# Keys and queries of a head group through one transposing transfer per token tile, and re-ordered first batches with causal masks added by TensorE

## The chip, the cores and the metric

The kernel runs on one core of a Trainium2 chip. The metric is the device time of one execution in microseconds; lower is better. In the profile PE is TensorE (PEld its weight loads), DVE VectorE, ACT ScalarE, POOL GpSimd, and SP the engine that issues most of the transfers. SPq and ACTq are the transfers issued by SP's and by ScalarE's queue. Each engine runs its instructions in program order.

## What is computed

Inputs: q, k, v of shape (8, 8, 576, 64): batches, heads, tokens, head width; s of shape (8, 8, 576); weights of 512 x 2048 and 2048 x 512.

```python
scores = scale * np.matmul(q, k.transpose(0, 1, 3, 2))
causal = np.triu(np.ones((S, S), dtype=bool), k=1)
cum = np.cumsum(np.maximum(s, 0.0), axis=-1)
bias = -(cum[:, :, :, None] - cum[:, :, None, :])
scores = np.where(causal, -1000000000.0, scores + np.minimum(bias, 0.0))
attn = softmax(scores)
x = matmul(attn, v)                  # heads side by side: (8, 576, 512)
xn = (x - mean) / sqrt(var + 1e-6) * g_ln
out = x + relu(xn @ w_ch1) @ w_ch2
```

## The kernel before

**Work.** There are 64 heads, n = 0 to 63 (n = 8 b + h). A head's scores are made transposed, keys on partitions, in three banks of 512 columns that hold only the blocks on and under the causal diagonal (`scores`, L300 to L336: tiles sa, sb, sc); the last block of 64 tokens is made for two heads at once (`scores_d`, tile sd). ScalarE takes Exp of each bank into the tile er (L314, L349). GpSimd then zeroes the upper half of each of the four diagonal blocks with an affine select (L328), and of the last block (L352). `pv` multiplies er with v and a column of ones (tile pot), and VectorE divides by the sum (L387 to L396). Layer norm (`ln_stats`, `ln_aggr`, `ln_xn`, `ln_tr`) and the two layers of the MLP (`mlp1`, tile ph, L467; `mlp2`, tile py, L485) of one batch run as 32 units between the heads of the next. The last 64 tokens of each batch are collected two batches to a tile (xm) for a last, mixed chunk.

**The bias by four more rows.** The contraction has 68 rows instead of 64: the cumulative sum, split into three bf16 parts c_hi, c_mid, c_lo, stands beside the keys, with ones beside them in the queries, and -c_hi beside the queries with ones in the keys.

**Keys and queries, two ways.** A group gam is 4 heads, half a batch; kT and qT have two buffers, used by groups in turn.
- Batches 0 and 1 (`NPE = 2`, groups 0 to 3): `load_qk` loads a pair of heads, `cast` makes bf16, `qk_pair` transposes on TensorE into PSUM (L261), and four copies take it to kT and qT (L113, VectorE). `aug` writes the bias rows with four small transfers.
- Batches 2 to 7 (groups 4 to 15): `ld_rows` loads token rows of a group (L213), `cast_rows` makes bf16 rows of 68 columns and 60 zeros on GpSimd (L230, L231), and `tr_rows` (L243) sends each tile of 128 or 64 tokens through a transposing transfer: one for K and one for Q for each of five token tiles, 512 columns each. The four parts of a group (K tiles 0 to 2, Q tiles 0 to 2, K tiles 3 and 4, Q tiles 3 and 4) are sent in the four heads before the group's first.

**Order.** Everything is written out by hand. In each head n: `pre(n)` (loads, casts and transposes due in this head), `qk_pair` where due, `scores(n)`, one MLP unit, `scores_d` on even heads, another unit, `pv(n-1)`, layer norm pieces, the rest of the units. Before the first head stands a setup: loads, fills, the cumulative sum, the first pair. The MLP starts with head 10, after the casts of its weights (`cast_w1` on VectorE, L160; `cast_w2` on GpSimd). SP issues loads, transposes and the output's stores in one queue, in program order; a transpose waits for its rows' cast, a store for its sum yo (L494), a load for a free buffer of its pool (2 each for K and Q, 3 for v).

Of the kernel before, what the change touches and what calls it, by code (L numbers as in the profile page):

```python
# [15 lines left out]
P = 128  # L16
# [3 lines left out]
def kernel(  # L20
# [26 lines left out]
    G = 4  # L47
    NPE = 2
    PARTS = ((0, 1, 2), (3, 4))
# [4 lines left out]
    stage = ctx.enter_context(tc.tile_pool(name="stage", bufs=2))  # L54
    pairs = ctx.enter_context(tc.tile_pool(name="pairs", bufs=3))
# [14 lines left out]
    ident = const.tile([P, P], BF16, name="ident")  # L70
    w1_bf = const.tile([P, KD, Dh], BF16, name="w1_bf")
# [5 lines left out]
    qT = [const.tile([P, G, SP], BF16, name=f"qT{i}") for i in range(2)]  # L77
    kT = [const.tile([P, G, SP], BF16, name=f"kT{i}") for i in range(2)]
    er = const.tile([P, 4, EW], BF16, name="er")
    rows = [const.tile([P, G, P], BF16, name=f"rows{i}") for i in range(6)]  # L80
    cTk = const.tile([P, NT, BH, 4], BF16, name="cTk")
    cTq = const.tile([P, NT, BH, 4], BF16, name="cTq")
    xm = [const.tile([P, Dm], F32, name=f"xm{i}") for i in range(4)]
    xTm = const.tile([P, KD, 512], BF16, name="xTm")
    ones4 = const.tile([G, S], BF16, name="ones4")
# [3 lines left out]
    c_neg = const.tile([BH, S], BF16, name="c_neg")  # L89

    def load_qk(src, b, j, name):
        tmp = stage.tile([P, 2, QT * D], F32, name=name, tag=name)
        nc.sync.dma_start(
            out=tmp[0:QP],
            in_=src[b, 2 * j : 2 * j + 2].rearrange("h (p t) d -> p h (t d)", t=QT),
        )
        return tmp

    def load_v(b, t):
        pn = P if t < NF else TL
        tmp = stage.tile([P, H, D], F32, name="vtmp", tag="vtmp", bufs=3)
        nc.sync.dma_start(
            out=tmp[:pn], in_=v[b, :, t * P : t * P + pn, :].rearrange("h s d -> s h d")
        )
        return tmp
# [8 lines left out]

    loaded = {}
    ready = {}

    def ld(kind, b, i):  # L120
        if b >= B:
            return
        if kind == "v":
            loaded["v", b, i] = load_v(b, i)
        else:
            loaded[kind, b, i] = load_qk(k if kind == "k" else q, b, i, kind + "tmp")

    def cast(kind, b, i, eng):
        if b >= B:
            return  # L130
        tmp = loaded.pop((kind, b, i))
        if kind == "v":
            pn = P if i < NF else TL
            copy_on(eng, v_bf[b % 2][:pn, i, :, 0:D], tmp[:pn])
        else:
            t = pairs.tile([P, QT, 2, D], BF16, name=kind + "p", tag=kind + "p")
            copy_on(
                eng,
                t[0:QP].rearrange("p t h d -> p h t d"),
                tmp[0:QP].rearrange("p h (t d) -> p h t d", d=D),  # L140
            )
            ready[kind, b, i] = t
# [32 lines left out]
    def cum_tile(name):  # L175
        return yop.tile([P, S], F32, name=name, tag="yo")

    def aug(b, g, eng):
        r0 = b * H + g * G
        i = (b * 2 + g) % 2  # L180
        for j, src in enumerate((c_hi, c_mid, c_lo)):
            eng.dma_start(out=kT[i][D + j : D + j + 1, :, 0:S], in_=src[r0 : r0 + G, :])
        eng.dma_start(out=qT[i][D + 3 : D + 4, :, 0:S], in_=c_neg[r0 : r0 + G, :])

    def bias_rows():
# [7 lines left out]
        for t0, t1, pn in ((0, NF, P), (NF, NT, TL)):  # L196
            nc.vector.tensor_copy(
                out=cTk[0:pn, t0:t1, :, 0:3],
                in_=tr[0:pn, :, t0:t1, :].rearrange("p j t x -> p t x j"),
            )  # L200
            nc.vector.tensor_scalar_mul(
                out=cTq[0:pn, t0:t1, :, 3], in0=tr[0:pn, 0, t0:t1, :], scalar1=-1.0
            )

    def ld_rows(kind, gam, part):
        if gam >= 2 * B:
            return
        src = k if kind == "k" else q
        b, h0 = gam // 2, (gam % 2) * G
        tmp = stage.tile([P, 3, G, D], F32, name=kind + "tmp", tag=kind + "tmp")  # L210
        for u, t in enumerate(PARTS[part]):
            pn = P if t < NF else TL
            nc.sync.dma_start(  # L213
                out=tmp[0:pn, u],
                in_=src[b, h0 : h0 + G, t * P : t * P + pn, :].rearrange("h s d -> s h d"),
            )
        loaded[kind, gam, part, "rows"] = tmp

    turn = [0]

    def cast_rows(kind, gam, part):
        if gam >= 2 * B:
            return
        tmp = loaded.pop((kind, gam, part, "rows"))
        got = []
        for u, t in enumerate(PARTS[part]):
            pn = P if t < NF else TL
            r = rows[turn[0] % 6]
            turn[0] += 1
            nc.gpsimd.tensor_copy(out=r[0:pn, :, 0:D], in_=tmp[0:pn, u])  # L230
            nc.gpsimd.tensor_copy(  # L231
                out=r[0:pn, :, D:KA],
                in_=(cTk if kind == "k" else cTq)[0:pn, t, gam * G : (gam + 1) * G, :],
            )
            got.append((t, pn, r))
        ready[kind, gam, part, "rows"] = got

    def tr_rows(kind, gam, part):
        if gam >= 2 * B:
            return  # L240
        dst = (kT if kind == "k" else qT)[gam % 2].rearrange("p h s -> p (h s)")
        for t, pn, r in ready.pop((kind, gam, part, "rows")):
            nc.sync.dma_start_transpose(  # L243
                out=dst[:, t * G * P : t * G * P + G * pn].rearrange(
                    "p (h s) -> p h s", h=G
                ),
                in_=r[0:pn].rearrange("p h c -> p (h c)"),
            )


    def qk_pair(b, j, engs=("dve", "dve", "dve", "dve")):
        if b >= B:
            return
# [3 lines left out]
        for kind, dst in (("k", kT), ("q", qT)):  # L257
            src = ready.pop((kind, b, j))
            tr = ps_t.tile([P, S], BF16, name="trqk", tag="tr")
            for t in range(QT):  # L260
                nc.tensor.transpose(  # L261
                    tr[:, t * QP : (t + 1) * QP],
                    src[0:QP, t, :, :],
                    ident[0:QP, 0:QP],
                )
            for u in range(2):
                copy_on(
                    engs[n],
                    dst[i][0:D, hh + u, 0:S].rearrange("d (p t) -> d p t", t=QT),
# [3 lines left out]

    def e_of(b, h):
        return er, h % 4


    def k_cols(b, h, kb):
        i, hh = (b * 2 + h // G) % 2, h % G
        if b < NPE:  # L280
            return kT[i][0:KA, hh, kb * P : (kb + 1) * P]
        n = P if kb < NF else TL
        o = kb * G * P + hh * n
        return kT[i].rearrange("p h s -> p (h s)")[0:KA, o : o + P]

    def q_cols(b, h, q0, q1):
        i, hh = (b * 2 + h // G) % 2, h % G
        if b < NPE:
            return [(q0, q1, qT[i][0:KA, hh, q0:q1])]
        flat = qT[i].rearrange("p h s -> p (h s)")  # L290
        got = []
        if q0 < NF * P:
            full = flat[0:KA, 0 : NF * G * P].rearrange("p (t h s) -> p t h s", t=NF, h=G)
# [242 lines left out]
    for t in range(3):  # L536
        ld("v", 0, t)
# [252 lines left out]
```

## Time and profile before

| | |
|---|---|
| median of three runs | 471.72 us (471.6 to 472.0) |
| profiled execution | 468.62 us |
| its span, first to last instruction | 466.9 us |
| mean granted TensorE clock | 0.893 |
| TensorE busy | 371.4 us (80%) |
| VectorE, ScalarE, GpSimd busy | 213.3, 175.4, 193.2 us |
| read from memory, written | 36.85 MB, 9.44 MB |

A row of a group reads: line, engine, operation, output and input tiles, shapes, count | busy time in us, mean ns of one | idle time of the engine before it, and what ended it. A row in order of time reads: start in us, duration, engine, line, operation, tiles, count [idle before, what ended it]. In the row of a transposing transfer grouped by line stand minimum, median and maximum in ns. A window's row reads: stretch, length, busy time (instructions) of PE, PEld, DVE, ACT and POOL, granted clock, share of the 16 transfer engines, GB/s. In the slices each digit is a tenth of busy time in a fortieth of the span; PEclk is the granted clock in tenths.

### The profile page before, as it was taken

What the parts mean: (1) busy time and instruction counts of PE and PEld (TensorE: products, weight loads), DVE (VectorE), ACT (ScalarE), POOL (GpSimd) and SP (SyncE); (2) the same over time, 40 slices, a digit from 0 to 9 for tenths busy, and PEclk for the clock granted to TensorE, in tenths of its full rate; (3) what the DMA queues carried; (4) which work ended last, traced back from release to release, by engine and by line L of the source; (5) the groups of instructions that cost most, each with busy time, mean ns of one, the idle gap of its engine ahead of it and who ended that gap; (6) DMA issues with size and microseconds to landing.
All of it is one profiled execution on the core that took longest, in us unless ns stands there. A gap on an engine that the chain in (4) does not pass through costs nothing. (4 is left out here: it accounts for less than half of the span.)

```text
span 466.9 us, 8307 instructions
## 1 busy us (share of the span) xinstructions
PE 371.4 (80%) x2848; PEld 200.3 (43%) x2895; DVE 213.3 (46%) x525; ACT 175.4 (38%) x339; POOL 193.2 (41%) x609
## 2 busy tenths in 40 slices
PE   1486469917979984999299939896699899999995
PEld 0264335504535542555155515453355455444442
DVE  7579777523714640447024712473145526511211
ACT  4252225603337242643255325532272463050320
POOL 3274516835646625554446545543466222000000
PEclk9975559987979995999789977999599999999999
DMA  7885078985877487665866586549765600101102
GB/s 201 216 249 138 13 251 241 217 181 137 191 146 139 97 176 169 115 129 119 189 135 132 117 196 131 117 103 174 162 133 107 137 2 22 69 0 46 46 23 68
DMA packets 167578, 61.09 MB, mean 131 GB/s; under 512 B 155624, under 2 KB 158768, under 8 KB 167536
## 3 DMA queue, kind: packets, MB, share of 16 engines
q1 hardware_dynamic: 167456, 60.51, 57.1%
q8 instruction: 23, 0.38, 0.4%
q14 instruction: 19, 0.16, 0.1%
q10 hardware_dynamic: 80, 0.05, 0.0%
HBM read 36.85 MB, written 9.44 MB: 99 GB/s over the span
## 5 line engine op out<-in xcount | busy, mean ns | idle before, releaser
L485 PE MATMUL py<-w_bf,hT 128*128 128x512 bf16 x554 | 135.6, 382 | 1.5 <-DVE yo L494 0.4
L467 PE MATMUL ph<-xT,w_bf 128*128 128x512 bf16 x488 | 130.3, 403 | 2.1 <-ACT hT L477 0.5
L328 POOL TENSOR_SCALAR_AFFINE_SELECT er<-er 128x128 bf16<-128x128 bf16 x256 | 73.4, 303 | 87.4 <-ACT er L314 86.9
L314 ACT ACTIVATE er<-sa 128x512 bf16<-128x512 f32 x64 | 38.1, 596 | 166.1 <-PE sa L305 107.3
L477 ACT ACTIVATE hT<-ph 128x512 bf16<-128x512 f32 x108 | 64.5, 597 | 91.9 <-PE ph L467 90.8
L467 PEld LDWEIGHTS <-w_bf 128*128 128x128 bf16 x576 | 53.9, 101 | 58.1 <-issue 11.3
L475 DVE TENSOR_SCALAR hT<-ph 128x512 bf16<-128x512 f32 x36 | 24.9, 692 | 113.7 <-PE ph L467 112.2
L305 PEld LDWEIGHTS <-kT 68*128 68x128 bf16 x464 | 35.8, 105 | 95.2 <-issue 38.2
L305 PE MATMUL sa<-qT,kT 68*128 68x512 bf16 x64 | 27.8, 434 | 60.2 <-DMA qT<-rows 47.3
L485 PEld LDWEIGHTS <-hT 128*128 128x128 bf16 x576 | 51.9, 98 | 50.2 <-issue 2.0
L379 PEld LDWEIGHTS <-er 128*128 128x128 bf16 x960 | 42.7, 105 | 17.9 <-issue 5.2
L379 PE MATMUL pot<-v_bf,er 128*128 128x65 bf16 x960 | 45.1, 203 | 3.2 <-POOL v_bf L115 2.5
L230 POOL CAST rows<-qtmp 128x256 bf16<-128x256 f32 (+1 forms) x60 | 24.1, 401 | 46.8 <-issue 25.1
L387 DVE RECIPROCAL rinv<-pot 128x5 f32<-128x5 f32 x64 | 12.4, 193 | 61.2 <-PE pot L379 61.0
L494 DVE TENSOR_TENSOR yo<-py,xb 128x512 f32<-128x512 f32 x32 | 22.0, 689 | 39.5 <-PE py L485 39.3
L314 ACT ACTIVATE er<-sc 128x512 bf16<-128x512 f32 x64 | 38.9, 608 | 0.0
L314 ACT ACTIVATE er<-sb 128x512 bf16<-128x512 f32 x64 | 38.2, 596 | 1.8 <-PE sb L305 0.7
L230 POOL CAST rows<-ktmp 128x256 bf16<-128x256 f32 (+1 forms) x60 | 23.9, 399 | 25.7 <-DMA kT<-rows 17.3
L305 PE MATMUL sb<-qT,kT 68*128 68x384 bf16 (+2 forms) x176 | 28.4, 269 | 2.5 <-DMA qT<-rows 2.3
L305 PE MATMUL sc<-qT,kT 68*128 68x256 bf16 (+1 forms) x224 | 28.5, 249 | 0.0
L389 DVE TENSOR_TENSOR xb<-pot,rinv 128x256 f32<-128x256 f32 x64 | 27.2, 424 | 2.2
L438 DVE TENSOR_SCALAR xn<-xb,mv,rs 128x512 bf16<-128x512 f32 x32 | 20.6, 704 | 9.7 <-POOL rs L425 9.7
(71 smaller groups left out, 289.8 us busy)
## 6 DMA issues: line engine op xcount, KB each, us to landing
vtmp<-in_v_dram SPq DMA_DIRECT2D x32, 256.0 KB
out_dram<-yo SPq DMA_DIRECT2D x32, 256.0 KB
ktmp<-in_k_dram SPq DMA_DIRECT2D x48, 128.0 KB
qtmp<-in_q_dram SPq DMA_DIRECT2D x48, 128.0 KB
w1tmp<-in_moe_w_ch_dram SPq DMA_DIRECT2D x8, 512.0 KB
w2tmp<-in_moe_w_ch_dram SPq DMA_DIRECT2D x8, 512.0 KB
ktmp<-in_k_dram SPq DMA_DIRECT2D x8, 288.0 KB
qtmp<-in_q_dram SPq DMA_DIRECT2D x8, 288.0 KB
```

Of the source, the lines that this page charges most:

```text
L230: nc.gpsimd.tensor_copy(out=r[0:pn, :, 0:D], in_=tmp[0:pn, u])
L305: nc.tensor.matmul(dst[:, a0 - q0 : a1 - q0], lhsT=k_cols(b, h, kb), rhs=cols, start=True, stop=True,)
L314: nc.scalar.activation(out=e[:, u, o : o + 512], in_=a, func=ACT.Exp, scale=scale)
L328: nc.gpsimd.affine_select(out=e[:, u, o : o + P], in_=e[:, u, o : o + P], compare_op=ALU.is_ge, fill=0.0, base=0, pattern=[[1, P]], channe ...
L379: nc.tensor.matmul(pot[:, t, :], lhsT=e[:, u, o : o + P], rhs=vv[:, kb, h, :], start=(kb == 0), stop=(kb == last),)
L389: nc.vector.tensor_tensor(out=xb[b][:, :, hs], in0=pot[:, 0:NF, 0:D], in1=rinv[:, 0:NF].unsqueeze(2).to_broadcast([P, NF, D]), op=ALU.mult,)
L438: nc.vector.tensor_scalar(out=xn, in0=x, scalar1=mv[:, t, 0:1], scalar2=rs[:, t : t + 1], op0=ALU.subtract, op1=ALU.mult,)
L467: nc.tensor.matmul(ph, lhsT=w1_bf[:, kd, fb * P : (fb + 1) * P], rhs=xT[:, kd, :], start=(kd == 0), stop=(kd == KD - 1),)
L475: nc.vector.tensor_scalar_max(out=hT[:, fb, :], in0=ph, scalar1=0.0)
L477: nc.scalar.activation(out=hT[:, fb, :], in_=ph, func=ACT.Relu)
L485: nc.tensor.matmul(py[0], lhsT=hT[:, fb, t * P : (t + 1) * P], rhs=w2_bf[:, fb, :], start=(fb == 0), stop=(fb == FB - 1),)
L494: nc.vector.tensor_add(out=yo, in0=py[0], in1=x)
```

## The change

1. kT and qT become one tile kq (K and Q side by side), and rows become tiles of K and Q side by side. One transfer per token tile transposes 1024 columns: five a group instead of ten. Row loads stay (one for K, one for Q per tile). GpSimd casts K and Q in one instruction, and copies the four bias columns of both in another. The transposes of a group are spread over the heads -4, -3 and -2 before its first (group 4: -3, -2, -1).
2. In the first ten heads (`NM = 10`) TensorE adds -1e30 above the diagonal by a product of the identity with a mask tile, four for each head, and the four affine selects of these heads go.
3. The first batches are re-ordered: one staging pool of six buffers for all loads; casts of pairs and of v almost all on GpSimd; one of the four pair copies on ScalarE; constant rows of ones and minus ones filled instead of transferred (c_hi is used for both operands, c_neg goes); the bias transfers of group 1 move from ScalarE's queue to SP's, that of g_ln from SP's to ScalarE's; an Exp of two numbers at the start.

```diff
+    NM = 10
+    NR = 4
-    stage = ctx.enter_context(tc.tile_pool(name="stage", bufs=2))
-    pairs = ctx.enter_context(tc.tile_pool(name="pairs", bufs=3))
+    stage = ctx.enter_context(tc.tile_pool(name="stage", bufs=6))
+    pairs = ctx.enter_context(tc.tile_pool(name="pairs", bufs=2))
...
+    kq = [const.tile([P, 2, G, SP], BF16, name=f"kq{i}") for i in range(2)]
-    rows = [const.tile([P, G, P], BF16, name=f"rows{i}") for i in range(6)]
+    rows = [const.tile([P, 2, G, P], BF16, name=f"rows{i}") for i in range(NR)]
...
+    def ld_rows(gam, t):
+        pn = P if t < NF else TL
+        b, h0 = gam // 2, (gam % 2) * G
+        tmp = stage.tile([P, 2, G, D], F32, name="rowtmp", tag="st")
+        for u, src in enumerate((k, q)):
+            nc.sync.dma_start(
+                out=tmp[0:pn, u],
+                in_=src[b, h0 : h0 + G, t * P : t * P + pn, :].rearrange("h s d -> s h d"),
+            )
+        loaded["rows", gam, t] = tmp
...
+    def cast_rows(gam, t):
...
+        nc.gpsimd.tensor_copy(out=r[0:pn, :, :, 0:D], in_=loaded.pop(("rows", gam, t))[0:pn])
+        nc.gpsimd.tensor_copy(
+            out=r[0:pn, :, :, D:KA], in_=cT[0:pn, t, :, gam * G : (gam + 1) * G, :]
+        )
...
+    def tr_rows(gam, t):
+        pn = P if t < NF else TL
+        r = ready.pop(("rows", gam, t))
+        o = t * 2 * G * P
+        nc.sync.dma_start_transpose(
+            out=kq[gam % 2]
+            .rearrange("p u h s -> p (u h s)")[:, o : o + 2 * G * pn]
+            .rearrange("p (h s) -> p h s", s=pn),
+            in_=r[0:pn].rearrange("p u h c -> p (u h c)"),
+        )
...
+    def aug(gam, eng):
+        r0 = gam * G
+        i = gam % 2
+        eng.dma_start(out=kq[i][D + 1 : D + 2, 0, :, 0:S], in_=c_hi[r0 : r0 + G, :])
+        eng.dma_start(out=kq[i][D : D + 1, 1, :, 0:S], in_=c_hi[r0 : r0 + G, :])
+        eng.dma_start(out=kq[i][D + 2 : D + 3, 0, :, 0:S], in_=c_mid[r0 : r0 + G, :])
+        eng.dma_start(out=kq[i][D + 3 : D + 4, 0, :, 0:S], in_=c_lo[r0 : r0 + G, :])
...
+        pe_mask = b * H + h < NM
+        def bank(name, blocks, o):
...
+                if pe_mask and diag:
+                    nc.tensor.matmul(
+                        a[:, c : c + P], lhsT=ident, rhs=maskT, start=False, stop=True
+                    )
+            nc.scalar.activation(out=e[:, o : o + 512], in_=a, func=ACT.Exp, scale=scale)
...
+        if pe_mask:
+            return
         for o in (0, OB + 64, OC, OC + 320):
             nc.gpsimd.affine_select(
...
+    nc.scalar.activation(out=warm[:, 1:2], in_=warm[:, 0:1], func=ACT.Exp)
+    nc.scalar.dma_start(out=gln, in_=moe_g_ln.rearrange("(kd p) -> p kd", p=P))
+    nc.gpsimd.memset(kq[0][D : D + 1, 0].bitcast(F32), NEG2)
+    nc.vector.memset(kq[0][D:KA, 1].bitcast(F32), ONE2)
...
+    cast_pair("k", 0, 0, "act")
+    cast_pair("q", 0, 0, "pool")
+    ld_v(0, 2)
+    ld_v(0, 3)
...
+    qk_pair(0, 0, ("act", "dve", "act", "dve"))
+    aug(0, nc.scalar)
+    cast_pair("k", 0, 1, "pool")
+    cast_pair("q", 0, 1, "pool")
+    ld_v(0, 4)
+    ld_pair("k", 0, 2)
+    ld_pair("q", 0, 2)
+    cast_v(0, 0, "act")
+    cast_v(0, 1, "pool")
+    ld_pair("k", 0, 3)
+    ld_pair("q", 0, 3)
     for i in range(2):
         nc.gpsimd.memset(v_bf[i][:, 0:NF, :, D : D + 1], 1.0)
...
+    cast_v(0, 2, "pool")
+    cast_v(0, 3, "pool")
+    cast_v(0, 4, "pool")
+    nc.gpsimd.memset(kq[1][D : D + 1, 0].bitcast(F32), NEG2)
+    nc.gpsimd.memset(kq[1][D:KA, 1].bitcast(F32), ONE2)
+    nc.gpsimd.memset(kq[1][0:KA, 0, :, S:SP], 0.0)
+    aug(1, nc.sync)
...
+        if n == 0:
+            cast_pair("k", 0, 2, "pool")
+            cast_pair("q", 0, 2, "pool")
+            ld_pair("k", 1, 0), ld_pair("q", 1, 0)
+            ld_v(1, 0), ld_v(1, 1)
...
+        lead = {2 * NPE: 1}
+        for gam in range(2 * NPE, NG):
+            m = n - 4 * gam - lead.get(gam, 0)
+            if m == -6:
+                ld_rows(gam, 0), ld_rows(gam, 1)
+            elif m == -5:
+                cast_rows(gam, 0), cast_rows(gam, 1)
+                ld_rows(gam, 2), ld_rows(gam, 3)
+            elif m == -4:
+                tr_rows(gam, 0), tr_rows(gam, 1)
+                cast_rows(gam, 2), cast_rows(gam, 3)
+                ld_rows(gam, 4)
+            elif m == -3:
+                tr_rows(gam, 2), tr_rows(gam, 3)
+                cast_rows(gam, 4)
+            elif m == -2:
+                tr_rows(gam, 4)
...
         if n >= 17:
+            if 1 <= h < 6:
+                ld_v(b + 1, h - 1)
+            if 2 <= h < 7:
+                cast_v(b + 1, h - 2, "pool")
...
+        if n == 0:
+            qk_pair(0, 1, ("dve", "dve", "dve", "act"))
+        elif h % 2 == 1 and n > 1 and n + 1 < NPE * H:
             g = (n + 1) // 2
+            qk_pair(g // 4, g % 4, ("dve", "dve", "dve", "act"))
         scores(b, h)
-        if n == 0:
-            qk_pair(0, 1)
```

409 lines of the change are left out of this document (138 added, 271 removed).

## The prediction

> **What bounds the kernel now.** I read the page first, then TensorE's instructions in order of time, then the SP queue in order of time, then the windows. On the page, TensorE is busiest, and its granted clock is near half in several slices.
>
> ```profile
> span 466.9 us, 8307 instructions
> PE 371.4 (80%) x2848; PEld 200.3 (43%) x2895; DVE 213.3 (46%) x525; ACT 175.4 (38%) x339; POOL 193.2 (41%) x609
> PE   1486469917979984999299939896699899999995
> PEclk9975559987979995999789977999599999999999
> DMA  7885078985877487665866586549765600101102
> ```
>
> The digits hide two regimes. From the fifth group of heads on (a group is 4 heads, half a batch; head n=16 is the first) keys and queries come through transposing transfers. In TensorE's rows, the first score of n=16, of n=20, and then of every eighth head after it:
>
> ```profile
> 105.56 0.59 PE L305 MATMUL sa<-qT,kT 68*128 68x512 bf16 x1 [10.22 <-DMA qT<-rows]
> 131.97 0.58 PE L305 MATMUL sa<-qT,kT 68*128 68x512 bf16 x1 [2.88 <-DMA qT<-rows]
> 181.16 0.59 PE L305 MATMUL sa<-qT,kT 68*128 68x512 bf16 x1 [8.28 <-DMA qT<-rows]
> 231.41 0.58 PE L305 MATMUL sa<-qT,kT 68*128 68x512 bf16 x1 [8.61 <-DMA qT<-rows]
> 279.46 0.59 PE L305 MATMUL sa<-qT,kT 68*128 68x512 bf16 x1 [7.04 <-DMA qT<-rows]
> 331.05 0.58 PE L305 MATMUL sa<-qT,kT 68*128 68x512 bf16 x1 [8.45 <-DMA qT<-rows]
> 338.18 0.38 PE L305 MATMUL sa<-qT,kT 68*128 68x512 bf16 x1
> 373.03 0.38 PE L305 MATMUL sa<-qT,kT 68*128 68x512 bf16 x1 [1.39 <-DMA qT<-rows]
> ```
>
> Once a batch TensorE stands for about 8 us until the last query transposes have landed. The first head after the stall takes 7.13 us (331.05 to 338.18); the next seven take 34.85 (to 373.03), 33.46 without the 1.39 of waiting, so 4.78 each. An undisturbed batch is 8 x 4.78 = 38.2 us. Five batches took 241.1 (131.97 to 373.03), 48.2 each. Why transfers are late is seen in SP's rows for one batch, first and last of 25 rows, with two transposing ones between, and the transposes grouped:
>
> ```profile
> 181.12 0.56 SPq L104 DMA_DIRECT2D vtmp<-in_v_dram  x1
> 181.78 3.84 SPq L243 DMA_TRANSPOSE kT<-rows  x3
> ...
> 194.56 2.48 SPq L243 DMA_TRANSPOSE kT<-rows  x2
> ...
> 230.18 1.25 SPq L213 DMA_DIRECT2D ktmp<-in_k_dram  x2
> ```
> ```profile
> L243 SPq DMA_TRANSPOSE kT<-rows x10: 1181/1203/2378, 181.8 to 223.4; - x10
> L243 SPq DMA_TRANSPOSE qT<-rows x10: 1186/1214/2339, 187.7 to 228.9; - x10
> ```
>
> The 25 rows sum to 44.9 us of the 50.3 us between two stalls: SP's queue is full, and 20 transposes are 28.3 of the 44.9. The queue sets the pace, not TensorE.
>
> **The change part by part.**
>
> *Transposes.* 20 a batch of 512 columns become 10 of 1024 columns. SP keeps 44.9 - 28.3 = 16.6 us of loads and stores (the row loads stay 20). What a double-width one costs on SP no row shows. It moves the same bytes in half as many pieces, so I bound it by 1.2 us (no growth) and 2.8 (twice the 28.3 / 20 = 1.41 of the present mean). The x3 row above is three 128-row pieces at 1.28 each; the x2 row is a 128-row and a 64-row piece at 1.24 each. Halving a piece leaves its price as it was, so the price is nearer a fixed one: I take 1.4. Then SP needs 16.6 + 14 = 30.6 us of a batch, below TensorE's 38.2, and TensorE becomes the bound. The transposes of a group are also issued in heads -4, -3 and -2 before its first, where now the last one comes in the head just before: two heads of slack (9 us).
>
> [...]
>
> *What hides the rest in this stage.* POOL casts keys and queries in one piece:
>
> ```profile
> L328 POOL TENSOR_SCALAR_AFFINE_SELECT er<-er 128x128 bf16<-128x128 bf16 x256 | 73.4, 303 | 87.4 <-ACT er L314 86.9
> L230 POOL CAST rows<-qtmp 128x256 bf16<-128x256 f32 (+1 forms) x60 | 24.1, 401 | 46.8 <-issue 25.1
> L115 POOL CAST v_bf<-vtmp 128x512 bf16<-128x512 f32 x29 | 17.5, 606 | 6.4 <-DMA vtmp<-in_v_dram 6.4
> L454 PE MATMUL trx<-ident,xn 128*128 128x128 bf16 x144 | 14.6, 229 | 10.7 <-DVE kT L113 7.8 <-DVE xT L459 1.4 <-DVE qT L113 0.9
> ```
>
> Two casts of 128x256 (0.80) become one of 128x512 (0.61), 120 casts become 60: some 12 us less on POOL, which is not the bound; costed at nothing. The windows say what else runs:
>
> ```profile
> 181.00:231.00 50.00, 40.82 (x334) 22.09 (x341) 21.17 (x58) 20.48 (x40) 24.69 (x82) 0.91 0.67 140
> 331.00:373.00 42.00, 40.24 (x330) 21.74 (x336) 19.12 (x53) 20.26 (x40) 21.34 (x72) 0.94 0.62 128
> ```
>
> POOL needs 24.7 us, DVE 21.2, ACT 20.5 of a batch: all fit in 38. The transfers' share, 0.67 of 50 us, is 33.5 us of the 16 engines. At a 38.2 us batch that is a share of 0.88, so I add 1.3 us of jitter and take 39.5. If a load comes late, POOL's cast waits in front of the masks of the next head; POOL's spare 14 us cover it. Five batches: 5 x (48.2 - 39.5) = 43.5 us. Heads 16 to 20: 26.4 us (105.56 to 131.97), at 4.9 a head 19.6, so 6.5 more. Sum for this stage 50 us.
>
> *First batches.* Their milestones: first scores of n=0, 4, 9 and 10, the first output product, and what stands on DVE and SP between n=9 and n=10; then the first second-layer product.
>
> ```profile
> 15.27 0.59 PE L305 MATMUL sa<-qT,kT 68*128 68x512 bf16 x1 [7.69 <-DMA qT<-c_neg]
> 28.81 0.44 PE L305 MATMUL sa<-qT,kT 68*128 68x512 bf16 x1 [1.51 <-DVE qT L113]
> 49.46 0.63 PE L305 MATMUL sa<-qT,kT 68*128 68x512 bf16 x1
> 64.43 0.63 PE L305 MATMUL sa<-qT,kT 68*128 68x512 bf16 x1
> ```
> ```profile
> 2.53 0.53 POOL L569 MEMSET v_bf<- 64x520 bf16 x1
> 19.76 0.58 ACTq L183 DMA_DIRECT2D qT<-c_neg  x1
> 20.39 0.60 ACT L314 ACTIVATE er<-sa 128x512 bf16<-128x512 f32 x1 [10.23 <-DVE qT L113]
> 22.40 1.03 PE L379 MATMUL pot<-v_bf,er 128*128 128x65 bf16 x15
> 52.03 3.94 DVE L438 TENSOR_SCALAR xn<-xb,mv,rs 128x512 bf16<-128x512 f32 x4 [1.14 <-POOL rs L425]
> 55.89 3.24 DVE L160 TENSOR_SCALAR w_bf<-w1tmp,gln 128x512 bf16<-128x512 f32 x8
> 56.79 2.74 SPq L150 DMA_DIRECT2D w1tmp<-in_moe_w_ch_dram  x4
> 59.06 1.51 DVE L113 COPY kT<-trqk 64x576 bf16<-64x576 bf16 x2
> 60.60 1.52 DVE L113 COPY qT<-trqk 64x576 bf16<-64x576 bf16 x2
> 88.37 1.03 PE L485 MATMUL py<-w_bf,hT 128*128 128x512 bf16 x4
> ```
>
> Added on TensorE: 40 mask products. The nearest row is the 128x128 transpose, 0.23 at most each: 9 us if nothing overlapped, less than half of it in a pipelined stream; it lies in heads where TensorE waits for other engines. Removed: 40 selects of 0.303, 12 us of POOL. But POOL gets all pair casts, and its setup grows by three fills of 1280 four-byte elements (estimate 1.3 us each, from 520 elements in 0.53). The bias transfers of the second group leave the ACT queue, where they hold the first Exp to 20.39; they go to SP, behind POOL's last fill (I count POOL there at 19 us), and with 4 x 0.6 us they hold the next batch's loads to about 21.5. The first Exp comes some 6 us earlier, yet the first output product also needs the select of the last diagonal block, which POOL reaches only behind those fills and two pair casts, at 21 us: against 22.40 now. So the early start is largely given back. After that DVE loses a quarter of its pair copies (3.03 of 59.06 to 62.1 for four) and pair casts, and POOL no longer stands between Exp and output: I take n=4 at 25.5 and n=9 at 42, 7.5 us earlier (bounds 0 and 15). Between n=9 and n=10 the DVE chain of 3.94 + 3.24 + 3.0 stays, less one copy of 0.75: n=10 at 56. The second half of the first weights is issued behind that chain (56.79 now, 48.5 then). From there to 88.37 is 31.6 us of streaming weights; I keep 32, so n=14 falls 7 to 8 us earlier. n=16, which now loses 10.22 more to its transposes, has them issued in heads 13 to 15 and loses perhaps 1: 8 + 9 = 17 us earlier. I take 16 (bounds 5 and 27).
>
> *The end*, from the last head on, is the same code and moves whole.
>
> Sum: 50 + 16 = 66. The profiled execution took 468.6 us (its span 466.9 and 1.7 around it): 468.6 - 66 = 402.6. The runs' median of 471.72 lies 3.1 above it, so **406 us**.
>
> **Rivals.**
> - *The transpose costs by width.* At 2.8 us each SP keeps its 44.9 us plus gaps, about 47 a batch: 5 x 1.2 = 6, heads 16 to 20 give 2, the start 14: 471.7 - 22 = 450. For it: nothing measured here excludes it in columns. Against: the price is flat in rows. Chance 0.12.
> - *The transfers' engines become the bound.* If they cannot hold more than a share of 0.78 in this mix, a batch takes 33.5 / 0.78 = 43: 5 x 5.2 = 26, 4 at heads 16 to 20, 14 at the start: 428. For it: many small pieces. Against: shares of 0.8 and 0.9 stand in the first third of the page. Chance 0.13.
> - *Slower.* One mechanism: a wide transpose holds SP so long that the row stage slows by more than the start wins. Equal pace is where 10 x + 16.6 + 2 = 48.2, x = 2.96 us; each further 0.1 costs 1 us a batch, 6 over the stage, so the 16 us of the start are used up at x = 3.25. At x = 3.6 it would be about 490. The largest single one in the rows is 2.4. Chance 0.05.
> - *It does little*, because the start loses what the row stage wins: within 0.2% of before, 0.02.
>
> **How the numbers follow.** The forecast case holds 0.68 and runs from 388 (batches of 38.2, a start 27 us earlier) to 420 (batches at 41.5, a start of 10). With the second rival the range reaches to 438; left out are the first rival, the slower case and a thin end below, 0.2. 0.2% is about what a measurement of this kernel can tell from no change. Faster 0.68 + 0.12 + 0.13 = 0.93, same 0.02, slower 0.05.
>
> **What would show it.** Right: in SP's rows a transpose median near 1.2 to 1.4 and gaps in its queue; no wait of TensorE on the transposed tile above 1 us after n=20; heads at 4.8 us; clock at full from n=20 on; transfers' share above 0.8; n=10 near 56 and n=16 near 89. Wrong: a median above 2; a wait on the rows' casts in POOL before each group; or n=10 as late as now because POOL's setup holds the first output product.

## The result, and the profile after

The changed kernel takes 419.8 us (417.0 to 421.4) against 471.7 (470.9 to 472.0): a ratio of 0.890 [0.885, 0.894], 52 us faster. The forecast was 406 in a range of 388 to 438: the time lies in the range, 14 us above the forecast. The profiled execution took 421.35 us, its span 419.5, 47.4 less than before.

In the kernel after, L282 is the score, L290 the mask product, L293 Exp, L301 the select, L351 the product with v; L94, L96 and L98 are the copies of ScalarE, VectorE and GpSimd; L146 loads rows, L129 v and L181 the first weights; L168 is `tr_rows`, L191 `cast_w1`, L158 the rows' cast, L410 `ln_xn`, L426 `ln_tr`. Rows of the page:

```profile
PE 366.0 (87%) x2888; PEld 201.7 (48%) x2935; DVE 198.1 (47%) x508; ACT 176.5 (42%) x345; POOL 172.9 (41%) x462
PE   1468718884899999999999999999999999999995
PEclk9985666999789999999999999999999999999999
DMA  7698029799989739974997699859966002002013
```

TensorE's busy time hardly changed (371.4 to 366.0); what went are its pauses. From the 12th slice to the last but one every digit of PE is 9, where before each batch had a dip. What is left of the trouble stands in the first eleven. TensorE's rows in order of time, the first scores of n=16, 20 and 60:

```profile
99.23 0.38 PE L282 MATMUL sa<-kq 68*128 68x512 bf16 x1
128.89 0.38 PE L282 MATMUL sa<-kq 68*128 68x512 bf16 x1
326.22 0.38 PE L282 MATMUL sa<-kq 68*128 68x512 bf16 x1
```

None of them waits (before: 10.22, 2.88 and 1.39 us). Set against the starts of the same heads before, the span divides so:

| stretch | before | after | gained | forecast |
|---|---|---|---|---|
| start to n=16 | 105.56 | 99.23 | 6.3 | 16 |
| n=16 to n=20 | 26.41 | 29.66 | -3.25 | 6.5 |
| n=20 to n=60, five batches | 241.06 | 197.33 | 43.7 | 43.5 |
| n=60 to the end | 93.87 | 93.28 | 0.6 | 0 |

The windows of the row stage (columns as before: busy time of PE, PEld, DVE, ACT, POOL, then granted clock, share of the transfer engines, GB/s), of the kernel before and of the one after:

```profile
132.00:373.00 241.00, 203.34 (x1658) 110.19 (x1689) 99.72 (x275) 101.77 (x200) 119.49 (x400) 0.90 0.67 139
```
```profile
128.90:326.20 197.30, 193.75 (x1659) 106.85 (x1688) 98.02 (x275) 99.80 (x200) 103.21 (x304) 1.00 0.80 170
```

TensorE is busy 193.75 of 197.30 us, at full clock: it is the bound here now. SP's transposes of the whole run, grouped:

```profile
L168 SPq DMA_TRANSPOSE kq<-rows x60: 1222/1268/3368, 88.7 to 320.9; - x60
```

SP's 164 rows in this stretch sum to 150.9 us, 30.2 a batch, and 50 transposes are 73.0 of it. The only waits of TensorE in the stretch, from the waits of that window (engine, line, what it waited for: us in all, times, longest):

```profile
PE pot L351 <- POOL er L301: 1.7, 3, 0.9
```

The start went otherwise. TensorE's, ScalarE's, VectorE's and SP's rows in order of time, of the kernel after:

```profile
16.43 0.61 PE L282 MATMUL sa<-kq 68*128 68x512 bf16 x1 [5.06 <-DMA kq<-c_lo]
17.18 0.60 ACT L293 ACTIVATE er<-sa 128x512 bf16<-128x512 f32 x1 [3.17 <-PE sa L290]
19.93 1.03 PE L351 MATMUL pot<-v_bf,er 128*128 128x65 bf16 x15
29.70 0.59 PE L282 MATMUL sa<-kq 68*128 68x512 bf16 x1 [3.58 <-ACT er L293]
44.99 2.30 DVE L96 COPY kq<-trqk 64x576 bf16<-64x576 bf16 x3
47.32 0.64 ACT L94 COPY kq<-trqk 64x576 bf16<-64x576 bf16 x1 [5.06 <-DVE kq L96]
47.98 0.60 ACT L293 ACTIVATE er<-sa 128x512 bf16<-128x512 f32 x1
48.63 0.46 PE L282 MATMUL sa<-kq 68*128 68x512 bf16 x1 [2.95 <-ACT er L293]
52.14 0.41 PE L282 MATMUL sa<-kq 68*128 68x512 bf16 x1
57.52 3.25 DVE L191 TENSOR_SCALAR w_bf<-w1tmp,gln 128x512 bf16<-128x512 f32 x8
58.42 2.74 SPq L181 DMA_DIRECT2D w1tmp<-in_moe_w_ch_dram  x4
60.69 2.29 DVE L96 COPY kq<-trqk 64x576 bf16<-64x576 bf16 x3
63.01 0.64 ACT L94 COPY kq<-trqk 64x576 bf16<-64x576 bf16 x1 [11.67 <-DVE kq L96]
65.18 0.63 PE L282 MATMUL sa<-kq 68*128 68x512 bf16 x1
```

The first score waits 5.06 us for c_lo, the last of the four bias transfers of the first group, and the first Exp starts at 17.18: 3.2 us earlier than before (20.39), not the 6 of the forecast. The first output product follows at 19.93 (forecast 21, before 22.40) without a wait of TensorE. But n=4 stands at 29.70, n=9 at 52.14 and n=10 at 65.18, all a little later than before (28.81, 49.46, 64.43). In front of n=8 there is a new chain: VectorE's three pair copies end at 47.29, the fourth copy on ScalarE starts at 47.32 after 5.06 us of waiting, the Exps of the head before stand behind it on ScalarE, and the next score waits 2.95 us for one of them. In front of n=10 ScalarE waits 11.67 us in the same way. Its whole in the waits of the kernel after:

```profile
ACT kq L94 <- DVE kq L96: 32.2, 6, 11.7
```

And in heads 16 to 20, rows of SP, TensorE and GpSimd, and the window:

```profile
99.49 1.13 SPq L129 DMA_DIRECT2D vtmp<-in_v_dram  x2
100.73 1.93 SPq L168 DMA_TRANSPOSE kq<-rows  x1
104.79 0.61 PE L282 MATMUL sb<-kq 68*128 68x64 bf16 x3 [5.19 <-DMA kq<-rows]
116.01 0.19 PE L351 MATMUL pot<-v_bf,er 128*128 128x65 bf16 x1 [2.07 <-POOL v_bf L98]
```
```profile
99.20:128.90 29.70, 22.02 (x171) 12.31 (x174) 12.62 (x38) 8.14 (x16) 17.30 (x44) 0.83 0.92 204
```

The last transpose of group 4 is issued at 100.73, inside the group's own first head, and TensorE waits 5.19 us for it; then 2.07 us for a tile of v. The granted clock is 0.83 over the stretch and the transfers' share 0.92, against 0.80 in the row stage.

### The profile page after: what moved, and what is told of

Read it like the earlier page. It is cut to its first block, busy times and chain, and to the rows that moved or that the text cites. A ratio compares the mean times of both kernels' runs of the same rounds, so it can differ in the third digit from the quotient of the medians.

```text
span 419.5 us, 8080 instructions
## 1 busy us (share of the span) xinstructions
PE 366.0 (87%) x2888; PEld 201.7 (48%) x2935; DVE 198.1 (47%) x508; ACT 176.5 (42%) x345; POOL 172.9 (41%) x462
## 4 chain that ended last, share of the span: by engine, by line
PE 59%; DVE 12%; DMA 10%; POOL 5%; issue 5%; SPq 4%; ACT 2%; POOLq 0%; ACTq 0%
PE ph L439 22%; PE py L457 19%; PE pot L351 7%; DMA vtmp<-in_v_dram 3%; DMA rowtmp<-in_q_dram 3%; DVE kq L96 3%; PE sc L282 3%; PE sb L282 3%; PE sa L282 3%; DVE xn L410 2%; SPq L168 2%; SPq L146 2%; DMA pairtmp<-in_k_dram 1%; ACT er L293 1%; PE trx L426 1%
## 5 line engine op out<-in xcount | busy, mean ns | idle before, releaser
L439 PE MATMUL ph<-xT,w_bf 128*128 128x512 bf16 x488 | 120.8, 381 | 4.3 <-ACT hT L449 2.5
L301 POOL TENSOR_SCALAR_AFFINE_SELECT er<-er 128x128 bf16<-128x128 bf16 x216 | 58.9, 297 | 39.1 <-ACT er L293 39.0
L293 ACT ACTIVATE er<-sa 128x512 bf16<-128x512 f32 x64 | 38.1, 595 | 86.5 <-PE sa L282 56.1
L282 PEld LDWEIGHTS <-kq 68*128 68x128 bf16 x464 | 37.0, 104 | 43.1 <-issue 5.6
L158 POOL CAST rows<-rowtmp 128x512 bf16<-128x512 f32 (+1 forms) x60 | 37.0, 616 | 45.2 <-DMA rowtmp<-in_q_dram 41.8
L351 PE MATMUL pot<-v_bf,er 128*128 128x65 bf16 x960 | 48.4, 200 | 4.2 <-POOL v_bf L98 2.1
L351 PEld LDWEIGHTS <-er 128*128 128x128 bf16 x960 | 42.0, 102 | 20.1 <-POOL er L301 5.5
L98 POOL CAST v_bf<-vtmp 128x512 bf16<-128x512 f32 (+1 forms) x39 | 23.9, 619 | 47.3 <-DMA vtmp<-in_v_dram 35.2
L293 ACT ACTIVATE er<-sb 128x512 bf16<-128x512 f32 x64 | 38.2, 596 | 5.2 <-PE sb L282 5.2
L293 ACT ACTIVATE er<-sc 128x512 bf16<-128x512 f32 x64 | 38.9, 608 | 0.2
L282 PE MATMUL sa<-kq 68*128 68x512 bf16 x64 | 26.9, 420 | 11.8 <-ACT er L293 6.5
L282 PE MATMUL sb<-kq 68*128 68x384 bf16 (+2 forms) x176 | 27.2, 260 | 5.2 <-DMA kq<-rows 5.2
L282 PE MATMUL sc<-kq 68*128 68x256 bf16 (+1 forms) x224 | 28.4, 242 | 0.0
L426 PE MATMUL trx<-ident,xn 128*128 128x128 bf16 x144 | 14.9, 231 | 10.5 <-DVE kq L96 8.6
```

What stands on the lines that cost most here:

```text
L98: nc.gpsimd.tensor_copy(out=out, in_=in_)
L158: nc.gpsimd.tensor_copy(out=r[0:pn, :, :, 0:D], in_=loaded.pop(("rows", gam, t))[0:pn])
L282: nc.tensor.matmul(a[:, c + a0 - q0 : c + a1 - q0], lhsT=k_cols(b, h, kb), rhs=cols, start=True, stop=not (pe_mask and diag),)
L293: nc.scalar.activation(out=e[:, o : o + 512], in_=a, func=ACT.Exp, scale=scale)
L301: nc.gpsimd.affine_select(out=e[:, o : o + P], in_=e[:, o : o + P], compare_op=ALU.is_ge, fill=0.0, base=0, pattern=[[1, P]], channel_mult ...
L351: nc.tensor.matmul(pot[:, t, :], lhsT=e[:, o : o + P], rhs=vv[:, kb, h, :], start=(kb == 0), stop=(kb == last),)
```

## Experiments: the row stage

The theory: SP's queue set the pace, and half as many transposes at the same price each set it free. Rivals: it is the earlier schedule (two heads of slack) that did it; or the price grows with width and something else paid for it.

**Two transfers of 512 columns** for each token tile, in the same heads.

```diff
-        nc.sync.dma_start_transpose(
-            out=...[:, o : o + 2 * G * pn]...
-            in_=r[0:pn].rearrange("p u h c -> p (u h c)"),
-        )
+        for u in range(2):
+            nc.sync.dma_start_transpose(
+                out=...[:, o + u * G * pn : o + (u + 1) * G * pn]...
+                in_=r[0:pn, u].rearrange("p h c -> p (h c)"),
+            )
```

> The kernel after, but K and Q of a token tile go through two transfers of 512 columns, in the same heads. If the queue's time for transposes is what the change took away, SP needs about 16.6 + 20 x 1.25 = 42 us and its gaps for a batch, so a batch goes from 39.5 to 44 to 48 us and the whole to 440 to 460. If instead the earlier heads in which they are issued made the gain, a batch stays at 39.5 to 40 and the whole within 5 us of 420.

Measured: 462.4 us (458.8 to 463.2), ratio to before 0.976 [0.971, 0.982]: four fifths of the gain are gone, and the whole lies 2 us above the range that was expected. Its transposes grouped, its window from n=20 to n=60, and TensorE's waits in that window:

```profile
L169 SPq DMA_TRANSPOSE kq<-rows x120: 1184/1247/2798, 87.8 to 365.9; - x120
```
```profile
135.20:367.40 232.20, 206.97 (x1659) 109.71 (x1688) 97.05 (x275) 99.69 (x200) 101.92 (x309) 0.97 0.66 145
```
```profile
PE pot L352 <- POOL er L302: 23.3, 14, 3.4
```

Five batches take 232.2 us, 46.4 each, against 48.2 before and 39.5 after. In the batch from n=36 to n=44 SP's rows sum to 44.8 of 46.6 us, 29.0 of them 20 transposes: the full queue of before, with the new order of the work around it. So the number of transposes is worth about 35 us (232.2 - 197.3), and the new schedule alone 9 (241.1 - 232.2). A reader should note where the full queue shows: not as a wait on the transposed tile, but as GpSimd's selects coming late, because the cast of a late load, mostly of v, stands in front of them. Rows of SP, GpSimd and TensorE for the longest of these waits:

```profile
213.83 6.07 SPq L169 DMA_TRANSPOSE kq<-rows  x4
219.96 0.57 SPq L129 DMA_DIRECT2D vtmp<-in_v_dram  x1
223.39 0.61 POOL L98 CAST v_bf<-vtmp 128x512 bf16<-128x512 f32 x1 [8.71 <-DMA vtmp<-in_v_dram]
224.30 0.79 PE L352 MATMUL pot<-v_bf,er 128*128 128x65 bf16 x9 [3.42 <-POOL er L302]
```

The load of v stands behind four transposes, its cast waits for the load, and the selects (L302) follow behind the cast.

**One head later**: all groups at the lead of group 4.

```diff
-        lead = {2 * NPE: 1}
+        lead = {g: 1 for g in range(2 * NPE, NG)}
```

> The kernel after, with loads, casts and transposes of every group one head later (the last transpose in the head just before the group, as in the kernel before; group 4 was so already). If the full queue was the cause, one head of slack is enough once the queue has room: batch 39.5 to 40.5, whole within 5 us of 420. If the slack of two heads carries the gain: a wait of some 5 us at each of 11 groups, 450 to 470.

Measured: 432.0 us (431.3 to 433.6), ratio 0.915 [0.912, 0.918]; five batches 211.6 us, 42.3 each: between the two cases that were expected. TensorE's waits from n=20 to n=60:

```profile
PE pot L351 <- POOL er L301: 8.6, 5, 3.3
PE sb L282 <- DMA kq<-rows: 4.6, 4, 1.8
```

So one head earlier is worth 14 us of the 43.7 here (211.6 - 197.3): a spare queue on average is not enough. A transpose in the head just before its use still comes late four times, for 4.6 us. The larger share, 8.6 us, are GpSimd's selects, in four of the five waits directly behind the cast of a late load of v. This edit moved loads, casts and transposes of the rows and left v where it was, so how much of the 14 us is slack of the transposes and how much the order of rows and v was not separated. Fewer transposes and the earlier place both count, and the prediction, which took the stage as one sum of issue times, priced them together.

**Transfers of 2048 columns**, two token tiles each, the fifth tile by itself: six transfers a batch instead of ten.

```diff
-    NR = 4
+    NR = 2
...
-    rows = [const.tile([P, 2, G, P], BF16, name=f"rows{i}") for i in range(NR)]
+    rows = [const.tile([P, 2, 2, G, P], BF16, name=f"rows{i}") for i in range(NR)]
...
+        if t < NF and t % 2 == 0:
+            return
+        t0 = t - 1 if t < NF else t
+        nt = t - t0 + 1
...
-            .rearrange("p u h s -> p (u h s)")[:, o : o + 2 * G * pn]
+            .rearrange("p u h s -> p (u h s)")[:, o : o + nt * 2 * G * pn]
```

> The kernel after, with two full token tiles in one transfer of 2048 columns: three transfers a group instead of five (two of 2048 columns, one of 1024 with 64 rows). It measures the price by width. If the price is fixed, the wide ones hold SP about 1.3 us; if it grows beyond some width, 2.0 to 2.6 us. The whole stays within 6 us of 420 by either, since TensorE bounds the stage.

Measured: 417.3 us (414.9 to 418.8), ratio 0.883 [0.878, 0.888], not to be told from the change itself (0.890 [0.885, 0.894]). Its transposes, and its window from n=20 to n=60:

```profile
L174 SPq DMA_TRANSPOSE kq<-rows x36: 1212/2058/4225, 86.1 to 314.6; - x36
```
```profile
126.20:321.00 194.80, 191.53 (x1659) 106.52 (x1688) 98.02 (x275) 99.55 (x200) 103.90 (x304) 1.00 0.81 173
```

TensorE was the bound already, so relief of SP brings nothing. The median of 36 mixes 24 wide transfers with 12 narrow ones of the fifth tile; in order of time a wide one and a narrow one read:

```profile
172.04 3.05 SPq L174 DMA_TRANSPOSE kq<-rows  x1
175.87 1.25 SPq L174 DMA_TRANSPOSE kq<-rows  x1
```

The 24 wide ones take 1.86 to 4.22 us, 2.73 in the mean (median 2.89). So the price is flat from 512 columns (median 1.25 us) to 1024 (1.27; mean 1.46), and from there to 2048 it about doubles: ten transfers a batch cost SP 14.6 us, four wide and two narrow ones 13.4 (4 x 2.73 + 2 x 1.25). Why the wide ones differ so much among themselves is not shown.

## Experiments: the start

**The change once more**, as the control of this set.

> The kernel after, unchanged, beside the next three on the same chip: 417 to 422 us, n=9 at 52, n=10 at 65, n=16 at 99 us.

Measured: 416.6 us (415.1 to 418.0), ratio 0.887 [0.883, 0.891]. n=4 at 28.2, n=9 at 50.6, n=10 at 63.7, n=16 at 96.1, n=20 at 125.8: the same pattern, 1.5 to 3 us earlier than in the first profile.

**No masks on TensorE**: the selects of GpSimd stay in all heads.

```diff
-    NM = 10
+    NM = 0
```

> The kernel after, with the masks of all heads by GpSimd's selects (NM = 0): 40 selects, 12 us, come back to GpSimd in the first ten heads, 40 small products leave TensorE. If the first heads are bound by the order of VectorE's copies and ScalarE's Exp, n=10 stays within 2 us of 65.2 and the whole is 416 to 424. If the masks on TensorE won time there, n=10 comes 5 us or more later and the whole is 425 or more.

Measured: 417.7 us (417.1 to 418.3), ratio 0.884 [0.881, 0.887]; n=9 at 51.3, n=10 at 63.0. The masks on TensorE bring nothing that can be measured. Windows of the first heads, of the control and of this kernel:

```profile
16.00:52.00 36.00, 26.34 (x278) 20.15 (x276) 18.83 (x52) 16.82 (x35) 13.42 (x24) 0.72 0.55 150
```
```profile
16.00:52.00 36.00, 26.11 (x241) 17.88 (x240) 18.56 (x50) 16.42 (x35) 23.19 (x61) 1.00 0.53 155
```

GpSimd does 9.8 us more, yet n=10 comes 0.7 us earlier: GpSimd's selects do not set the pace of the first heads, and 40 products fewer on TensorE gain next to nothing. The two figures of the clock, 0.72 and 1.00, can't be compared. A stretch without a clock record counts as full clock, and the trace of this kernel holds no record before 66.6 us, that of the control none before 21.9. The first score product of a head took as long in both windows (control first; minimum, median, maximum in ns):

```profile
L282 PE MATMUL sa<-kq x9: 376/615/627, 16.7 to 50.6; 68*128 68x512 bf16 x9
```
```profile
L282 PE MATMUL sa<-kq x10: 582/616/628, 15.5 to 51.3; 68*128 68x512 bf16 x10
```

At full clock (1.00 in the row stage) it takes 0.38 us, as at n=16, n=20 and n=60 above, so TensorE was slow in both. The next two kernels try the copies of the pairs.

**ScalarE's copy first.** In the pair copies, the one on ScalarE is the first of the four instead of the last.

```diff
-            qk_pair(0, 1, ("dve", "dve", "dve", "act"))
+            qk_pair(0, 1, ("act", "dve", "dve", "dve"))
...
-            qk_pair(g // 4, g % 4, ("dve", "dve", "dve", "act"))
+            qk_pair(g // 4, g % 4, ("act", "dve", "dve", "dve"))
```

> The kernel after, with ScalarE making the first of the four pair copies instead of the last. In the kernel after ScalarE's copy starts only when VectorE's third copy has ended, and the Exps of the same head stand behind it. If that order holds the first heads up, the Exps of n=3, 5 and 7 come 2 us earlier each, n=9 at 46 to 49 instead of 52, and the whole is 413 to 417. If VectorE's work bounds these heads anyway, n=9 stays at 51 to 53 and the whole at 418 to 422.

Measured: 411.7 us (408.8 to 413.7), ratio 0.876 [0.870, 0.882]; the control's interval lies just above it. Rows of ScalarE, VectorE and TensorE in order of time:

```profile
39.73 0.63 ACT L94 COPY kq<-trqk 64x576 bf16<-64x576 bf16 x1 [0.60 <-PE trqk L239]
40.42 0.60 ACT L293 ACTIVATE er<-sa 128x512 bf16<-128x512 f32 x1
41.97 2.33 DVE L96 COPY kq<-trqk 64x576 bf16<-64x576 bf16 x3
43.76 0.58 PE L282 MATMUL sa<-kq 68*128 68x512 bf16 x1 [2.37 <-DMA kq<-c_mid]
```

ScalarE's copy no longer waits for VectorE, the Exps follow at once, and n=8 starts at 43.8 instead of 47.1 (control); what its score waits for now is a bias transfer. n=4 at 27.0, n=9 at 47.3, n=10 at 60.6, n=16 at 90.2, so 5.9 us earlier than the control; of these 4.8 stay in the median.

**No copy on ScalarE**: all four on VectorE, as before the change.

```diff
-            qk_pair(0, 1, ("dve", "dve", "dve", "act"))
+            qk_pair(0, 1, ("dve", "dve", "dve", "dve"))
...
-            qk_pair(g // 4, g % 4, ("dve", "dve", "dve", "act"))
+            qk_pair(g // 4, g % 4, ("dve", "dve", "dve", "dve"))
```

> The kernel after, with all four pair copies on VectorE, as in the kernel before: VectorE does 0.77 us more for each pair, ScalarE waits for none of it. By the first theory (the Exps are held up behind the copy) n=9 at 47 to 50 and the whole 414 to 419; if VectorE bounds these heads, n=9 at 54 to 56 and the whole 421 to 425.

Measured: 413.6 us (412.7 to 414.5), ratio 0.881 [0.878, 0.884]; n=9 at 47.8, n=10 at 61.7, n=16 at 92.0. Its runs lie below all of the control's, though the intervals touch. Giving ScalarE the last copy was worse than giving it none; giving it the first looks a little better than none, by less than the two intervals tell apart. Either way the first heads gain: n=16 comes 5.9 us earlier with the copy first and 4.1 without it.

**First weights earlier.** VectorE's chain between n=9 and n=10 holds the second half of the first weights (issued at 58.42). Their casts are spread over heads 6 to 10, first on GpSimd, then, in a second kernel, on VectorE.

```diff
-            nc.vector.tensor_scalar_mul(
+            nc.gpsimd.tensor_scalar_mul(
...
             ld_pair("k", 1, 2), ld_pair("q", 1, 2)
+            cast_w1(0), ld_w1(4)
...
             cast_v(1, 4, "pool")
+            cast_w1(1), ld_w1(5)
+            cast_w1(2), ld_w1(6)
...
             cast_pair("q", 1, 1, "pool")
+            cast_w1(3), ld_w1(7)
         elif n == 9:
-            for i in range(4):
-                cast_w1(i)
-                ld_w1(4 + i)
+            cast_w1(4), ld_w2(0)
+            cast_w1(5), ld_w2(1)
...
```

> The kernel after, with the first-layer weights cast on GpSimd from head 6 on instead of on VectorE from head 9 on, and every later weight load and cast one to three heads earlier. In the kernel after the transfers' engines stand nearly still from 40 to 58 us, because the second half of these weights waits for casts behind the layer norm on VectorE, and from 65 to 120 us they are full. If that hole is what cost the first stage its gain, n=10 comes 3 us earlier, n=20 at 112 to 120 instead of 129, and the whole is 404 to 412. If GpSimd's longer work or TensorE bounds the heads 10 to 20, n=20 stays above 125 and the whole above 415.

Measured: 413.5 us (412.3 to 414.6), ratio 0.881 [0.877, 0.884]; n=10 at 62.0, n=16 at 93.5, n=20 at 122.1: 3 us, between the two cases that were expected. The casts grouped (minimum, median, maximum in ns; first and last start), in the kernel after and in this one:

```profile
L191 DVE TENSOR_SCALAR w_bf<-w1tmp,gln x16: 475/477/567, 57.5 to 72.5; 128x512 bf16<-128x512 f32 x16
```
```profile
L191 POOL TENSOR_SCALAR w_bf<-w1tmp,gln x16: 1554/1556/1716, 32.7 to 66.7; 128x512 bf16<-128x512 f32 x16
```

A cast with a factor takes GpSimd 1.56 us where VectorE needs 0.48. That spreads the casts over 34 us, so part of the head start was lost in this experiment's own cost.

> As the run with the weights cast earlier on GpSimd, where each of these casts took 1.55 us and held the loads back itself; here they stay on VectorE (0.41 us each), eight of them in heads 6 to 8, which has room there (17 of 36 us busy). If the hole in the transfers from 45 to 55 us is what costs the heads 10 to 20, the second half of the first weights is loading from 40 us on, n=10 comes at 60 to 62, n=16 at 86 to 92, n=20 at 112 to 118, the whole 404 to 410. If the heads are bound otherwise, n=20 stays above 122 and the whole above 413.

Measured, with the first two lines of the diff left out (casts on VectorE): 414.7 us (414.1 to 415.7), ratio 0.879 [0.875, 0.882]; n=10 at 63.8, n=16 at 96.1, n=20 at 123.0. The window of the former gap, of the kernel after and of this one:

```profile
45.00:65.00 20.00, 7.58 (x93) 6.22 (x91) 14.93 (x40) 5.89 (x12) 3.32 (x5) 0.67 0.23 63
```
```profile
45.00:65.00 20.00, 9.53 (x83) 7.25 (x84) 15.62 (x41) 6.69 (x14) 3.05 (x4) 0.50 0.50 155
```

The gap in the transfers is half filled (share 0.23 to 0.50), and n=16 does not come earlier for it (control 96.1). That the missing time of the start lay in the late weights has fallen; they give some 2 us, and those in heads 16 to 20. With the casts on GpSimd n=16 came 2.6 us earlier than in the control, which speaks for the time that VectorE then had free, not for the weights.

## Experiments: heads 16 to 20

**Group 4 without its later start**, so that its last transpose is issued a head earlier.

```diff
-        lead = {2 * NPE: 1}
+        lead = {}
```

> The kernel after, with group 4 scheduled like all others, one head earlier. In the kernel after, the last transpose of group 4 (head 15) stands in SP's queue behind six loads, and TensorE waits 5.2 us for it in n=16 and then runs at half clock. If that order is the cause, the wait goes, n=17 comes 5 us after n=16 instead of 11.6, and the whole is 410 to 415; if the transfers are simply full there, the time returns as later weights or v, n=20 stays within 2 us of 126 and the whole within 3 us of 417.

Measured: 417.8 us (416.1 to 419.1), ratio 0.885 [0.881, 0.889]: no change. The wait of 5.19 us is gone, n=17 follows n=16 after 6.5 us instead of 11.7, but n=16 itself comes 3 us later than in the control (99.1 against 96.1; no single wait accounts for it), and in the next head TensorE stands for a tile of v:

```profile
113.55 0.22 PE L351 MATMUL pot<-v_bf,er 128*128 128x65 bf16 x1 [3.86 <-POOL v_bf L98]
```

**Half of the second weights**: only four of its eight loads are made.

```diff
     def ld_w2(i):
+        if i >= 4:
+            return
...
     def cast_w2(i):
-        nc.gpsimd.tensor_copy(out=w2_bf[:, 2 * i : 2 * i + 2, :], in_=loaded.pop(("w2", i)))
+        src = loaded.pop(("w2", i)) if i < 4 else w2_bf[:, 2 * i - 8 : 2 * i - 6, :]
+        nc.gpsimd.tensor_copy(out=w2_bf[:, 2 * i : 2 * i + 2, :], in_=src)
```

> The kernel after, but only the first half of the second-layer weights is loaded; the second half is copied from the first on GpSimd, so that part of the product is not computed: 2.1 MB fewer to load between heads 12 and 15, all else as before. If full transfers are what slows the heads 14 to 20 (shares of 0.9 to 1.0 from 85 to 115 us), those 2.1 MB are worth 2.1 MB / 220 GB/s = 9.5 us, n=20 comes at 115 to 120 instead of 126 and the whole at 406 to 411. If the order in SP's or GpSimd's queue slows them, n=20 stays at 124 to 127 and the whole at 415 to 420.

Measured: 413.5 us (412.4 to 413.9), ratio 0.875 [0.871, 0.879]; n=16 at 96.5, n=20 at 122.4. The stretch takes 25.9 us, 3.8 less than in the kernel after, not the 9.5 that 2.1 MB were priced at; n=20 and the whole lie between the two cases that were expected. The wait on the rows falls to 0.19 us, and v is late again; SP issues its load at 105.78, and TensorE waits:

```profile
109.42 0.21 PE L354 MATMUL pot<-v_bf,er 128*128 128x65 bf16 x1 [4.25 <-POOL v_bf L98]
```

The megabytes of the weights are then not the whole cause, nor is the place of group 4's transposes. In both kernels TensorE still loses some 4 us in this stretch to a tile of v, and 2.07 and 0.75 us more to GpSimd's selects; the granted clock of the stretch is 0.94 and 0.87. When all groups were issued one head later, the stretch was shorter too (98.4 to 123.6), with 2.27 us of waiting for the rows and 3.11 for v. There less of group 5 stood in front of group 4's last transpose, which would fit the shorter wait for the rows; v came no earlier, and none of this is shown by a run of its own. What would settle it, v's loads of batch 2 pulled ahead of the rows, was not tried.

**Three together**: ScalarE's copy first, the first weights earlier on VectorE, group 4 without its later start.

> Three edits of the kernel after together: ScalarE's copy first, the first-layer weights earlier on VectorE, group 4 one head earlier. If they act in different places, their gains add: 5 for the copy, 6 to 10 for the weights, 2 to 5 for the group: 396 to 405 us. If one limit (full transfers from 65 to 125 us) stands behind all, the sum saturates at 405 to 410.

Measured: 410.2 us (409.7 to 411.3), ratio 0.870 [0.866, 0.874]; n=10 at 60.6, n=16 at 93.1, n=17 at 96.9, n=20 at 118.6. It beats both kernels, the change by some 2%, and is not to be told from ScalarE's copy first alone (0.876 [0.870, 0.882]). The gains do not add: n=16 comes 2.9 us later than with ScalarE's copy first alone (90.2), and TensorE again stands for v, now in the second head of the stretch.

```profile
104.58 0.21 PE L351 MATMUL pot<-v_bf,er 128*128 128x65 bf16 x1 [3.71 <-POOL v_bf L98]
```

## Why the prediction was right, and where its sum was off

**The row stage was right, in cause and size.** 43.7 us against 43.5. The price of a wide transpose, the one number that no row showed, was taken as 1.4; its median is 1.27 and its mean over the stage 1.46 (73.0 / 50). SP needs 30.2 us a batch (30.6 was worked out), TensorE is the bound at 39.5 (39.5), the clock is full. The transfers' share is 0.80, at the edge of what was named and below the 0.85 that the sum implied. The rivals by width and by the transfer engines fell with these rows. What the sum did not separate is the slack: with one head less it would have been 42.3 a batch, near the second rival's 43 for another reason. And the 1.3 us of jitter a batch were a guess: TensorE is idle 0.7 us a batch (197.3 - 193.75, over five) and busy 38.75, where 38.2 was worked out. That the two errors cancel to 0.2 us in 43.7 is luck.

**Mis-sized: the start, 16 us forecast, 6.3 measured.** The failing step is the one that counted VectorE's lost fourth copy as a gain of 0.75 us and costed nothing on the engine it moved to. ScalarE took it in program order in front of the Exps of a head (the last mask product on the first of these banks had ended at 43.83, and its Exp started at 47.98, behind the copy), and it started only when VectorE's third copy was done. Put first, it takes 5.9 us off the start; 3.1 more of the 9.7 that are missing at n=16 are the difference between two executions of the same kernel, the one profiled first and the control (99.23 and 96.1). With the copy first n=16 stands at 90.2 (forecast 89), but that it comes so near is in part luck: the forecast of n=4, 9 and 10 (25.5, 42, 56) stays too early even then (27.0, 47.3, 60.6), and the six heads from n=10 take 29.6 us where 33 was forecast. The difference before n=9, some 5 us, is not traced to a single wait. The other half of the reason given, that POOL's fills hold the first output product, is near in its number (19.93 against 21) and wrong in its cause: the select did come behind the fills, at 20.17, but TensorE did not wait for it. What had held it was c_lo, the bias transfer in front of its first score.

**Mis-sized: heads 16 to 20, 6.5 us forecast as a gain, 3.25 measured as a loss.** The step took them at 4.9 us a head as soon as the transposes were fewer, and let group 4's transposes, issued in heads 13 to 15, cost perhaps 1 us in front of n=16. Measured are 5.19 us of waiting for the group's last transpose inside n=16, 2.07 for v, and heads 17 and 18 at 6.6 and 6.7 us (110.97, 117.61, 124.32 are the starts of 17, 18 and 19). The sum of the SP queue was made for a steady batch and not for this stretch, in which row loads, transposes, v and stores meet right after the weights. The cause of what remains is open, as said above.

**Sum.** The start and these heads lack 9.7 and 9.75 us; the row stage and the end gave 0.8 more: 18.7. The profiled execution of the change lay 1.6 above its median where the forecast, after the kernel before, had allowed for 3.1 below it, so 14 are left between 406 and 419.8. Two sums of the prediction are slightly off and change nothing in this: 26.4 less 19.6 is 6.8 and not 6.5, and the upper end of its forecast case comes to 422 and not 420.

## What to carry to other kernels

When a queue is full, count its instructions before its bytes: halving the number of transfers at the same bytes was worth 35 us here, and making them wider still nothing, since by then another engine was the bound. When a copy is given to an engine to relieve another, look at what stands behind it in the new engine's order and what it must wait for: one copy of 0.64 us, at the wrong end of a list, cost 5 us. And work out the issue queue for the transition into a steady state by itself; its sum for the steady state says nothing of it.

## What the runs showed of the hardware

- A transposing transfer holds SP's queue for 1.25 us at 512 columns, 1.27 at 1024 (medians), and for 2.73 at 2048 (mean of 24, which range from 1.86 to 4.22).
- A cast with a factor per partition, 128x512, takes GpSimd 1.56 us and VectorE 0.48, while GpSimd's plain cast of that shape takes 0.61.
- ScalarE's copy out of the transposed pair started 0.03 us after VectorE's third copy ended (47.29 and 47.32 above), although the two read different partitions of their tile and write different columns of kq. Whether it is the tile read or the tile written that ties them was not separated; another order removes the wait.
- In the first heads a 68x512 score product took 0.62 us (medians of 0.615 and 0.616) with the 40 mask products and without them, against 0.38 in the row stage, at a clock of 1.00. The view's clock of 1.00 without them comes from a stretch of the trace that holds no clock record; of the four executions of that kernel three show a mean clock of 0.985 to 0.987 and one 0.942, all within 417.1 to 418.3 us. In the row stage the clock was 0.90 before, where TensorE was busy 203.34 of 241.00 us, and 1.00 after, where it was busy 193.75 of 197.30; no run shows what sets the clock.
